# Attention with a gated MLP on one core: two more key blocks on VectorE, and another written-out order

## The chip, the core and the metric

The kernel runs on one core of a Trainium2 chip. Four compute engines work in parallel, each through its own in-order queue of instructions: TensorE (PE) multiplies matrices, ScalarE (ACT) computes exponentials, VectorE (DVE) and GpSimd (POOL) do elementwise work; SyncE (SP) issues transfers. The metric is the device time of one execution in microseconds. The time before is 680.48 us, the median of three runs (678.22 to 682.14).

## The reference

The input is x, 2048 rows of 512 values in bf16. After a layer norm, two branches are computed and added to x:

```python
xn = layernorm(x)
# A: attention, 32 heads of 16
q, k, v = heads(xn @ wqkv)
p = softmax(q @ k.T / 4)          # 2048 x 2048 for each head
A = (p @ v) @ wo
# B: gated MLP, 1792 wide
gate, up = xn @ W_gate, xn @ W_up
B = (gate * (gate > 0) * up) @ W_down
out = x + A + B
```

The attention has 32 x 2048 x 2048 exponentials, 134 million. They are the bulk of the elementwise work.

## The kernel before

**Tiles.** Queries are taken in 4 chunks of 512 (c4), heads in 4 groups of 8 (gg), and each group in two sets of 4 heads (ee). That gives 32 blocks. For each block the keys run in 16 key blocks of 128 (kt), so there are 512 key blocks in all, and each holds 4 heads x 128 keys x 512 queries of scores.

**TensorE in halves.** Nearly all matmuls are 64 rows by 32 columns of the array. A "half operation" is four such matmuls side by side on one half of the rows (lines 260 to 266); two half operations, one on each half, can run at once. Ahead of it stand its four weight loads. While the program is emitted (lines 404 to 411), the weights that each half holds are tracked: where the next half operation on the same half has the same weights (`wkey`), its loads are left out. The scores of one key block on one half share their weights (keys), and so do the products with V of the same key block on one half.

**Two ways to compute an exponential.** A key block on ACT takes 4 score half operations, into two pairs of PSUM banks that are reserved for this, two ACT instructions on 128 x 1024 values (line 1420, one "unit" each, `ring<-ps`), and two half operations on V. A key block on DVE (`quad`, line 1367 on) takes 4 score half operations into the four shared PSUM banks, four DVE instructions that add a bias and round to int16 (line 1375, `qd<-ps`), which makes the raw bit pattern of a bf16 number close to the exponential, and two more patterns of the same size, shifted by a constant, whose sum with the first comes nearer to the exponential. Each shift is one DVE instruction on 128 x 2048 values (line 1394) or two pieces on GpSimd (line 1390). All three patterns are multiplied with V, so there are six half operations on V. Raw tiles have 4 buffers, patterns 5. Scores of a key block on DVE are asked for up to 10 units ahead.

The table `QUAD_AT` has a row for each of the 32 blocks and a character for each of its 16 key blocks: a dot means ACT, a digit DVE. The digit says which shifts go to GpSimd: 0 neither, 1 the first, 2 the second, 3 both. There are 159 digits, so 353 key blocks are on ACT: 706 units. The first two blocks are done by halves: key blocks 0 to 7 of each, then 8 to 15 of each.

**Everything else** stands in the background: projections for Q, K and V, the MLP (`glu`, its products evicted at lines 1059 and 1063), and the output rows (`out_rows`). Its PSUM banks are the four shared ones. After each block its sums are copied (line 1253), inverted, and multiplied in on GpSimd (lines 1282 and 1287).

**The order.** Nothing is scheduled at run time. `PLAN` is a compressed list with one entry for each operation in the order in which all engines' queues are filled, and the buffer that each takes. `PLAN_OPS` is its length, 8302. `Graph.run` (line 339) replays it. A wait is put in wherever an operation needs one of another engine, and each engine's queue is in order: behind an instruction that waits, the rest of that queue waits too.

Of the kernel before, what the change touches and what calls it, by code (L numbers as in the profile page):

```python
# [16 lines left out]
S = 2048  # L17
D = 512
H = 32
DH = 16  # L20
F = 1792
# [3 lines left out]
NB = 4  # L25
NGG = 4
VW = 18
VN = 17
# [41 lines left out]
    ".0....3.....2...",  # L70
    ".3...3...2...3..",
# [15 lines left out]
    "3.2.3..3..2..3..",  # L87
# [32 lines left out]
NHS = 20  # L120


PLAN_OPS = 8302
PLAN = (
    "c-mcC2|!F;8@}(kGt)Fpi&QGv_dSuNLPGXPSraW}7fEHwPJ}Fd5`~n|A|X-8k}b-<@0GG;-;$Yo|8vg0cgp{vnmcECm*;)n=bY(dn1BD{$v<BDiF}b>kv|Pz;vX9_FNGh(3B2$g`71o;|5=b{s-HD@h5s?H#BHkQ"
    "OH=53;%?Qu>I@LRG<d}`4T|X;PJG0HWQS-mr!$=w=YnLYZcUyCX(wq9U^rm}(6xpCIELo{|DoeJG6d*;934V_=ER-oL{9eu-jtZela25{o)?3`>4K`WLo}8{{|1E2!n-qcJD#jZCz1yowHr8TM_w|Pz9a+bmOOCM"
    "hWHsLx=UVBk3>Itx+KpD+Y*m}r+(qE(HF!DAcpYNEi#(UqF!+%jvOP!NX&;A5*kYV-@>NUO<sJH;b<K3roam?$euzRr5N*!?x_%S;KYCn`Jsl9VDn<e=`)TlPUlKF=4h}$T!H!lf|;C<Bq7Ok4dS5|1WUzbsE>jX"
    "!XOeb2@!$^)Bz0=tQ1F(eMJkzh?1}L4Z$~tcq+avB3aD7XuA|D3F90iMutwrfT7RCN)<NNGGgSA7KwPLai$Z+y~qr$7*Ga8_l3|QI#gU=OfnuTI`~gQbmb-$U(KT9#6rWE77ZlmCMIzbWI(J_4u_itMVvukN47yi"
    "Qs@uWb%-doiFabgwLF8!7%j;I2O#<^*iV)t?*EmOy`^9XB!L7wc>E6j!_(p;Ka$`G!IKz8M44c;7Id6}?Z%ta$7D5%WFdTXDH>$0SSut~!p=0_40$4^jf6;-907O&P<bIvya+n{PlK@M0x(4EFf`?KJD%DuvH{rz"
    "n<^xm(=A4$i?^hX;D5wzPK=tsDx#IVt_R>?&{fEHvIp4-KV=XH61iw8m(cmVNP_~vNYMYt$eUV$+=KvYbsQpA6U~PRB914~$HV9o9<M_q#fu(_-1$dAfP<YOE@%;n7k(4xk(Lf8)HOAqM`8d;HiYa776@xmx2PrL"  # L130
    "J4aKA<4iXc!A)lgcoo+bs88Tc3_OBB0hvNX@fR(529<hZPKkx$It06wN*WKbNC=!+Y!Y6Hghw1nCXva%<%mW{h=O1$b&Yt&i<#yncxjP{UYbO$Fo!3sz)?EJjsq?@p^C9p40(x24bti)6-#&H88Ll$9+JvNs0x9L"
# [1345 lines left out]
```

## Time and profile before

| what | value |
|---|---|
| runs, median (lowest to highest) | 680.48 us (678.22 to 682.14) |
| profiled execution | 675.45 us |
| its span in the trace | 673.5 us |
| busy: PE, ACT, DVE, POOL | 666.5, 656.0, 616.3, 512.5 us |
| weight loads (PEld) | 381.7 us, 21226 instructions |
| matmuls | 22358 |
| granted TensorE clock | 1.0 |

The profiled execution was 5 us quicker than the median run. In the profile's lines a group is named by line, engine and operation, what it writes and reads, its shape and count; behind the bar stand its busy time in us and the mean of one in ns, and after the second bar the idle time of the engine just before it with what ended it. The mean of one counts from start to end; instructions of an engine overlap at their ends, so busy time divided by count is the step from one to the next. In the windows there is, for each engine, busy time and in brackets the number of instructions.

### The profile page before, as it was taken

What the parts mean: (1) busy time and instruction counts of PE and PEld (TensorE: products, weight loads), DVE (VectorE), ACT (ScalarE), POOL (GpSimd) and SP (SyncE); (2) the same over time, 40 slices, a digit from 0 to 9 for tenths busy, and PEclk for the clock granted to TensorE, in tenths of its full rate; (3) what the DMA queues carried; (4) which work ended last, traced back from release to release, by engine and by line L of the source; (5) the groups of instructions that cost most, each with busy time, mean ns of one, the idle gap of its engine ahead of it and who ended that gap; (6) DMA issues with size and microseconds to landing.
All of it is one profiled execution on the core that took longest, in us unless ns stands there. A gap on an engine that the chain in (4) does not pass through costs nothing.

```text
span 673.5 us, 46743 instructions
## 1 busy us (share of the span) xinstructions
PE 666.5 (99%) x22358; PEld 381.7 (57%) x21226; DVE 616.3 (92%) x1042; ACT 656.0 (97%) x718; POOL 512.5 (76%) x519
## 2 busy tenths in 40 slices
PE   8999999999999999999999999999999999999998
PEld 4545655555565556555556655565565565565554
DVE  8958889999999999989999989998999899999894
ACT  6999999999999999999999999999999999999995
POOL 3322676787788788897788877898988888898883
PEclk9999999999999999999999999999999999999999
DMA  7330121112321111112110102111121212111111
GB/s 219 52 76 24 53 64 36 42 47 79 82 80 49 52 39 37 53 51 72 47 47 23 47 5 73 25 52 52 46 58 43 55 30 55 43 32 50 46 50 49
DMA packets 57806, 35.96 MB, mean 53 GB/s; under 512 B 21196, under 2 KB 53644, under 8 KB 57612
## 3 DMA queue, kind: packets, MB, share of 16 engines
q1 hardware_dynamic: 57324, 32.72, 18.0%
q8 instruction: 170, 2.79, 1.6%
q10 hardware_dynamic: 288, 0.26, 0.1%
q14 instruction: 24, 0.20, 0.1%
HBM read 26.35 MB, written 2.35 MB: 43 GB/s over the span
## 4 chain that ended last, share of the span: by engine, by line
PE 94%; DVE 4%; DMA 1%; POOL 0%; issue 0%; ACT 0%; SPq 0%
PE ps L264 94%; DVE stats L760 1%; DVE xn_sb L773 1%; DMA xnT<-xn_sb 1%; DMA x_sb<-in_A_x_dram 0%; DVE v_aug L911 0%; DVE qT L987 0%; DVE qd L1375 0%; DVE xnT L814 0%; DVE kT L904 0%; DVE mv L761 0%; POOL rstd L755 0%; ACT xn_sb L1219 0%; DVE kT L1001 0%; SPq L689 0%
## 5 line engine op out<-in xcount | busy, mean ns | idle before, releaser
L1420 ACT ACTIVATE ring<-ps 128x1024 bf16<-128x1024 f32 x706 | 649.7, 1129 | 2.9 <-PE ps L264 2.5
L1390 POOL TENSOR_TENSOR qd<-qd,ints 128x512 int32<-128x512 int32 x458 | 462.5, 1041 | 124.9 <-DVE qd L1394 59.3
L264 PE MATMUL ps<-qT,kT 64*32 64x512 bf16 x8192 | 458.7, 374 | 0.2
L1375 DVE TENSOR_SCALAR qd<-ps 128x512 int16<-128x512 f32 x636 | 412.0, 685 | 33.5 <-PE ps L264 29.3
L264 PE MATMUL ps<-qd,v_aug 64*32 64x512 bf16 x3816 | 302.0, 375 | 0.0
L264 PE MATMUL ps<-ring,v_aug 64*32 64x512 bf16 x2824 | 242.3, 375 | 1.4 <-DVE kT L904 1.4
L1355 PEld LDWEIGHTS <-kT 64*32 64x32 bf16 x7944 | 163.8, 92 | 105.1 <-issue 14.9
L1327 PEld LDWEIGHTS <-v_aug 64*32 64x32 bf16 x5756 | 138.5, 91 | 73.4 <-issue 11.4
L264 PE MATMUL ps<-xnT,wgs 64*32 64x512 bf16 x1792 | 140.5, 374 | 0.0
L264 PE MATMUL ps<-xnT,wus 64*32 64x512 bf16 x1792 | 137.2, 374 | 0.0
L1394 DVE TENSOR_SCALAR qd<-qd 128x2048 int16<-128x2048 int16 x89 | 63.2, 715 | 0.5 <-PE ps L264 0.2
L844 PEld LDWEIGHTS <-wgs 64*32 64x32 bf16 x1792 | 43.0, 91 | 23.7 <-issue 3.5
L844 PEld LDWEIGHTS <-wus 64*32 64x32 bf16 x1792 | 43.1, 91 | 23.3 <-issue 2.1
L264 PE MATMUL ps<-Wd,hT 64*32 64x512 bf16 x608 | 54.5, 375 | 0.0
L844 PEld LDWEIGHTS <-hT 64*32 64x32 bf16 x1440 | 34.7, 92 | 19.8 <-issue 1.4
L264 PE MATMUL ps<-Wo_p,x_sb 64*32 64x512 bf16 x480 | 42.8, 375 | 0.0
L264 PE MATMUL ps<-Wv,hT 64*32 64x512 bf16 x448 | 40.9, 375 | 0.0
L1059 DVE COPY up_sb<-ps 128x512 f32<-128x512 f32 x56 | 38.3, 683 | 1.4 <-PE ps L264 0.7
L264 PE MATMUL ps<-xnT,Wq 64*32 64x512 bf16 x480 | 36.6, 375 | 0.2
L264 PE MATMUL ps<-Wv,xnT 64*32 64x512 bf16 x576 | 36.3, 374 | 0.1
L264 PE MATMUL ps<-Wk,hT 64*32 64x512 bf16 x384 | 35.5, 375 | 0.0
L264 PE MATMUL ps<-xnT,Wk 64*32 64x512 bf16 x480 | 34.0, 374 | 0.4 <-DMA xnT<-xn_sb 0.2
(73 smaller groups left out, 308.3 us busy)
## 6 DMA issues: line engine op xcount, KB each, us to landing
rb<-rec_scr SPq DMA_DIRECT2D x124, 64.0 KB, 2.2
wus<-in_B_W_up_dram SPq DMA_DIRECT2D x38, 128.0 KB, 2.8
wgs<-in_B_W_gate_dram SPq DMA_DIRECT2D x38, 128.0 KB, 2.9
xr_sb<-in_A_x_dram SPq DMA_DIRECT2D x16, 128.0 KB, 2.6
qT<-qf SPq DMA_DIRECT2D x120, 16.0 KB, 1.9
out_dram<-xn_sb SPq DMA_DIRECT2D x14, 128.0 KB, 2.3
x_sb<-in_A_x_dram SPq DMA_DIRECT2D x8, 128.0 KB, 2.9
x_sb<-oT SPq DMA_DIRECT2D x60, 16.0 KB, 2.0
```

Source lines behind the costliest of these rows:

```text
L264: return e.add_instruction(mybir.InstMatmult(name=e.bass.get_next_instruction_name(), engine=mybir.EngineType.PE, ins=[e.lower_ap(x), e.lo ...
L760: G.op("DVE", 580, lambda e, m=m: e.bn_stats(stats[:, m, :], xs(m)), reads=[t_xm[m]], writes=[t_st], prio=pr, order=last_xn if m == 4 else ())
L773: G.op("DVE", 320, lambda e, m=m, t=t_n: e.tensor_scalar(xn_sb[:, t.slot, :], xs(m), mv[:, m, 0:1], rstd[:, m:m + 1], op0=ALU.subtract, op ...
L844: e.ldweights(w()[rows, 32 * j:32 * j + 32], tile_position=(rows.start, 32 * j))
L1059: G.op("DVE", 603, lambda e: e.tensor_copy(up_sb[:, tup.slot, :], bank_of(tu)), reads=[tu], writes=[tup], prio=-590)
L1327: e.ldweights(vs(j), tile_position=(64 * half, 32 * j))
L1355: e.ldweights(ks(m), tile_position=(64 * half, 32 * m))
L1375: G.op("DVE", 601, lambda e, j=j, tx=tx: e.tensor_scalar(qd[:, tq.slot, 512 * j:512 * j + 512], ps[:, BANK[tx.slot], :], IBIAS[3], 0.0, op ...
L1390: G.op("POOL", POOL_NS / POOL_PIECES + 60, lambda e, x=x, n=n, c=slice(i * m, i * m + m): e.tensor_tensor(x().bitcast(I32)[:, c], raw().bi ...
L1394: G.op("DVE", 600, lambda e, n=n, x=x: e.tensor_scalar(x(), raw(), float(SHIFTS[n + 1]), None, op0=ALU.add), reads=[ti, tq], writes=[t], p ...
L1420: exp_ops[u] = G.op("ACT", 904, lambda e, tr=tr, k0=k0: e.activation(ring[:, tr.slot, :, :], ps[:, 4 * k0:4 * k0 + 2, :], ACTF.Exp, scale= ...
```

## The change

Two key blocks move from ACT to DVE (161 digits instead of 159, 351 key blocks on ACT, 702 units): key block 9 of block 1 and key block 7 of block 2. In block 18, key block 0 goes to ACT and key block 15 goes to DVE in its place, with one of its shifts on DVE where both were on GpSimd. The order in `PLAN` is another one throughout, with half operations of the same weights side by side more often: 1650 weight loads fewer are issued. Nothing else differs.

```diff
 QUAD_AT = (
     "................",
-    ".0....3.....2...",
-    ".3...3...2...3..",
+    ".0....3..2..2...",
+    ".3...3.2.2...3..",
     "2...3..3..0..3..",
...
     "2...3..3..0..3..",
-    "3.2.3..3..2..3..",
+    "..2.3..3..2..3.2",
     "2...2..3..0..3..",
...
-PLAN_OPS = 8302
+PLAN_OPS = 8319
 PLAN = (
...
```

More of the change, by code (lines that the diff above doesn't have):

```diff
@@ new lines @@
+    "c-m!K2S82l`#;ZnPPf}_ku+4cFIgFp8A(<p(jucMlD@K|j4xlw$S7G+D#}VInThNfg?#OujO<al_niOxzUQ2K^ZU1)&Uwc(KF{ZQp7(@d{`?Tgw;*4UAM$VHv++}W*_e4MUPu!J@frCNZwr4cC@{Kvjh^9e=9#pO"
+    "ZoWK)K9hDMAH1|LF!B}xSwvtOJ=fll#!9OQ+9mN1K_|igY$h<gG>XSxAjq51(c}xXIxzwdbc8@g;%WFdG8XWsv<kT=2=qQR7>J7jPq*L^nNF|7T|fhL44zJI3HTNgBwZOvA@UOm(j@62Sw$3*h)izqqLl<97NfnU"
+    "tJ6EO8a&;O3QL6pt<ON~AUsA8l^~k{S%@Lm^jqM?&4KPs1fmPl*+gy78cOFELB^6Gn^KS`>a5I5-;#L+x(oHUAnC$TF&IWeE~(L}n8eIlZ1Lhx(I|9=AkeW?D{)J*D-n?VrePRKO>rJiEs39K=x84PKWgZLl9B=v"
@@ new lines @@
+    "_hRT>QD@1Z8Y;3JJ46+p0!G}1ItD}|NGK9b!i(sko)b03Gt{gICh8~I4m^dBEI4(Tel>LvFIktkTgDC|vS>i7kcOI+ZZE=uNKQdbp-GjZKoEuDDKJ5U#3@KrlR^TCD5W@|Na4j8lJF_T6_rPjBUkj309u5LI24U0"
+    "&=}Lmp@PU3)Y=RZRiy}^>uV6b7N|tL0NT*kkg>8GMOPF3MVJ$}X+(L5T^L@9YwA=gEl5jJ?Zl@VVgVW2R10hj2{Ir)kTk?2#egBk6HQKk;@ugf0WGy^M9UFTM0I!yOwpQxXb@uI8V(7%fT27=Y(h04a|KB*1{e+K"
+    "sEur(!8=N{CTO%VDWj5()&OQ9@c{`2VryPTq-0=<Q?f7iKQBkHC>|o<q~<|*C{-PpDt(bGY6&E<A>jf!4n?UM(W`=n3QBh*R%NKMHAvzIvbGpkcn5kZ?k5w!XiIuqltd6&kE}*5CXy6ZMRFerL145)=&E!L4Rt=X"
@@ new lines @@
+    "n}k1XYzh;)rKG&P9i!cfF851G89@+r#iKRU`gkG(lx&bL#c6P8YGgQ&u`;5tDaaxex(xY7(sNz}HugldQbI$OzBb=!NOGav#8U&*7FRM6zD+?*9tp&2yh!21#nkB{SVdTgL?j_V40sSE_mI_z^dj_l5-U;+X^<G8"
+    "L|joB7E2{6PR9OHl50XUB(%h}#f*d`3Z?uaCu@zEK&fL8Pvs=?^TeQ{%91z51!!c5K_sRqX_!cVI35`!azB!`C49zc6_tw(jhMh?d`Lp6SwTub;s6@_f)*Xrz%)0KF>0X2ia>)^12Q|1tqGYk+LXb7nv?Si2!9kV"
+    "QltuU0+Dl{n4al<yq1VVDjAlQC4@`)lEPk$Il2=STdEqw3@g<%BFR%r@v;>Jt%Ou~neHeuDduI|syQ)gkX#*V8D1uKZ6zh830V_u6(IakJ4#xJ55%fR${0wORip|*hBmdo6a_$vEU^v}A%)}=fV34NS(BI3pPZ;g"
@@ new lines @@
+    "x+km3$&H~~NI9JcnbL&X1*TjJ$ZCtUEr<rkqp4x!GPHJyENI;-Q@c#uf?VcFGeFMt+LBZPsRRNVxr~%`CASa?5c46AWV@220Rk^mDg!i&@^bYiR(DcC!fW9n5YneI$oOQmaV8hlf=*aTj#`2WwLC4zMaCcXE$HgP"
+    "TD5@a0=dl9tuM<WbC)2dCK|=Owh-1<u+qw)p&3Og9lse<I*_tHwF6;1(O1;*JkrL!6wxw(c_cZ9*NXntxR!&oqT*S<Ik7yX7#6)H@+Z{{;duh1>pG~VWw6Nm$??HUSP;aD4&;_aswQQ!VHho9<wij)8pYH?D<rW_"
+    "BCN>Bl@owiNl27S%_Q+3uT6zw5)_ai<p9bENM~5F2;j9frXW{<bT3)}A)U5jvLZDx66ADA30q1E{8tmH!V#knNsbb2D8oUE5}IIti}{^aZxW};D5ai6YFR-+td=Bh6bTb2eW_|B{zBRki4pUNh5;SbP@<8lL)u#~"
@@ new lines @@
+    "Vj%wJNR=V?L|V|)B18#K64>N2PA>n61vMfXkXX}V+u%isvv{%51Ce&5SeNKoW?;E$q!tk&A~h9^+&kCmeu&B-*3V*(Ct6ZkM35O$%)XLVj99^m*wQkZ)cjHB@>&T+QsL!JNNkm~fh0Dd+P0dP1O_qQBm>FqnjkGK"
+    "r*F}X3|*WTLrd)4<W^tH$f7t>e=C*OQgI_642VF`-qA>HsAMZC3`Hf#_8L}O?2C4gcwgI1%j}N{K$<2yhS<CIISH?=$+a8m+$5eb2x9m3(G&^Va+*d1qNTeS<CL$Yy=e<Z&l2Ql!<7>!Rr|DIqD6~D7=lKJ3^_(c"
+    "Xi8RPpjshux0pQCpgq%(K%-0ef-V;@x{^RLopjAh4|u6bmC_RfteO{e<&U<Xl6zx8N5r&LrB7sz7x5%8AI!w)q75KMtrSM2b^)=CAnAv8?$X%=Pcyzq0NQR^cQ_%s6}0H6T}g<QFeBqz;&#b-w6)Y$1oH8LmbtX2"
@@ new lines @@
+    "Q*sT!Xc=9QPCaTL!_~^BLalQYX$v0dR+ba2cv7H4npEt`uBQATww|=-BPxpBzqXPRv<<a*Qbi*Tq*Nf6G1`8L5u0jWEHb1R0I_Wrv~9E8v1-q9wC-kT2A26)jdYcRAeJ<>C|^F;(;d`7E#%2Hn6^6>YT2CE6(@Wx"
+    "@9?^Fzgo#&d&~lIHig=ix=43OE(65?mup^Hf@mc2;VGkwXIV(QtjJ`v<fR7$QtyZZgC*^b)bEL&r}Z9>q*@S3<f=Q*k_s%bTceGqM#?FI3~NNoc2P}w`lu^TMWuhJMBU$7NF_h}XW6PNxc{d`k&!0UI;xdUQ*>vj"
+    "y7NHYQ7+BYQjtr91-@3tDrim5Gum!KTL4QZA-D%Yz-x1}sJ^7Gm<UA#5+DkkTF#a_8A%mGnpu$`c}DDb7^!`x&nYA&nirix`Io0Hy>t?x0Ua6AN{B(?DFF|EG&cgT;drUv)*hQ6B7s1OiXKJKQa}&`LOLYiC6=bW"
@@ new lines @@
+    "4brl=RQB`o=^{-Rv~xjHCY2Ar#70LRCmn|h^065sm;N&K$thZwz-7csZGt>p;%8Y^UhMGHthTCPbS=GHxXR$cHWVu=?NKs0mqgmi4hg#G(l(;nj^PhT$-IUHoOI>GK3#g}C1c7*)S|c=B%dw9Z^Veq4st^+%ETaD"
+    "6D~KPf7Iqu11X|TJbx9%7Ar=XbU=ILC!RV0Bh=;^=@gRo^tDPCTBXZ{g^vB1+VKTiv3SV}Jo872snwbb+Qt+9w<)dNuQ57Sma72ybY1QkCGOYOh|<|TFC}Hk@q+eDUyuq!=`0-Na)^i8g&&0g67y{B_f0z4cwN`2"
+    ">roh})qZQ!!k?!K+BXjW({2j7HxBZdvY>5K<eKM?bqF!a4%Bjy?yQ5Um97Or_#@rFYM?t8;X(I?ftLb9#wW1~FTIlz$ql53+CY<%xgZu&@(DM6A%be*QpzBr))H~cOay<tjggZ&BlDf0Jr$Gd27wpXV8p}B+ApaX"
@@ new lines @@
+    "-MhS6uX`BX>o?J<jG*lhbT9IRTCf&sl|0&4Tz|aLgIWolul=4y7adYM*S)gTzI)_l`wEgd<x>PkJ|3@qPR>gw;*zms<)o@#B5BFkbPcUKB=*HpQ9`U(YU|DqNgW_HG>rIyO73uZsRI`^l_4s7OD#2e@Ml>g=$igN"
+    "xJo`Y(4C_(wN7$s6;iTQ<X4SyveOQb&ZxDO@gGzuJB`=9aizC^bG2U;)FKxtF0==F+Lw@0fyT%+6!X6wfqVol_ZGDe9BcL3wK@={)(M=vrojB~dt+XQ!diD3zP6UNjLHbLDiVqHbYPZphj_LsmqhT#yD#~$n!ep*"
+    "YNs=%Rztw($V+>?$o%=DTL4{y$@~#Ug4R>oV=Ns5YSn{3^wwrT>8-M$BU1UrATO&_``x@aT>Gk5E3TNkYJJJ?rkL8!V(P)4A1@T3`27P|Kmuw5EYGt1l@1(dP|flNHPGoAr_Z*6o6xZY^vQ4wPNT2EUy8d;xrYes"
@@ L229 @@
+    "qY|SL&!A-#)`57IET+%UvW?6#)gzWyQ1$>??vV5*6)P+yLFygC9wr=31PrY$h{;HuhKndd5F8<X>Ia;Cz!<NuhaIgTo3Nl{34`DurEVa(9Ak;4#R8dOOv@n!OZ;raQY*8jv}gj#8-&&<N=b=ImM{ccVs}$)8Y5~V"
+    "hSQ^K5WX~^<p9<Q?C>BHnshNw5GtYNE3IOQrA!D%(b^LuP(_q5AZY@Tk^+Omh!nAu;3)GbNF0&-Dk>7LZHQ56Q9?!-lE_DlxfLzP2o9;tN?ZfbD5TCKg%(zdTo9z-=eWvIC@dNfBT{mvV;Sl@3M-Zo*@k8X01*j5"
+    "Qm=y6wHzfX2E>8|vHu6m;-IP")
 class Pool:
```

177 lines of the change are left out of this document (75 added, 102 removed).

## The prediction

> **What bounds the kernel now.** First the page: the totals and the costliest groups.
>
> ```profile
> span 673.5 us, 46743 instructions
> PE 666.5 (99%) x22358; PEld 381.7 (57%) x21226; DVE 616.3 (92%) x1042; ACT 656.0 (97%) x718; POOL 512.5 (76%) x519
> L1420 ACT ACTIVATE ring<-ps 128x1024 bf16<-128x1024 f32 x706 | 649.7, 1129 | 2.9 <-PE ps L264 2.5
> L1390 POOL TENSOR_TENSOR qd<-qd,ints 128x512 int32<-128x512 int32 x458 | 462.5, 1041 | 124.9 <-DVE qd L1394 59.3
> L264 PE MATMUL ps<-qT,kT 64*32 64x512 bf16 x8192 | 458.7, 374 | 0.2
> L1375 DVE TENSOR_SCALAR qd<-ps 128x512 int16<-128x512 f32 x636 | 412.0, 685 | 33.5 <-PE ps L264 29.3
> L264 PE MATMUL ps<-qd,v_aug 64*32 64x512 bf16 x3816 | 302.0, 375 | 0.0
> L264 PE MATMUL ps<-ring,v_aug 64*32 64x512 bf16 x2824 | 242.3, 375 | 1.4 <-DVE kT L904 1.4
> L1355 PEld LDWEIGHTS <-kT 64*32 64x32 bf16 x7944 | 163.8, 92 | 105.1 <-issue 14.9
> L1327 PEld LDWEIGHTS <-v_aug 64*32 64x32 bf16 x5756 | 138.5, 91 | 73.4 <-issue 11.4
> L1394 DVE TENSOR_SCALAR qd<-qd 128x2048 int16<-128x2048 int16 x89 | 63.2, 715 | 0.5 <-PE ps L264 0.2
> ```
>
> PE's 99% cannot be taken at its word, because ends of matmuls are modelled. ACT's 97% can: 706 exponentials fill 649.7 us, 0.920 us each, and ACT stands idle ahead of them for 2.9 us in the whole run. (The mean of 1129 ns overlaps with the next one; the step is what counts.) So I read ACT's timeline next, at both ends and in a quiet place.
>
> ```profile
> 11.65 13.25 ACT L1420 ACTIVATE ring<-ps 128x1024 bf16<-128x1024 f32 x14
> ...
> 299.27 4.70 ACT L1420 ACTIVATE ring<-ps 128x1024 bf16<-128x1024 f32 x5
> 299.27 5.61 ACT L1420 ACTIVATE ring<-ps 128x1024 bf16<-128x1024 f32 x6
> ...
> 649.43 14.91 ACT L1420 ACTIVATE ring<-ps 128x1024 bf16<-128x1024 f32 x16
> ```
>
> The exponentials run from 11.65 to 649.43 + 14.91 = 664.34, that is 652.7 us. Undisturbed, one more costs 5.61 - 4.70 = 0.91 us, so 706 of them need 642.5 us. What PE's lateness adds is 652.7 - 642.5 = 10.2 us in all. The rest of the span, 11.65 us ahead and 9.2 us behind, is start and tail. **ACT is the bound; PE takes the second place.** How near PE is, the timeline of its two row halves and the windows tell.
>
> ```profile
> 301.60 0.38 PE L264 MATMUL ps<-ring,v_aug 64*32 64x512 bf16 x4
> 301.61 0.38 PE L264 MATMUL ps<-qT,kT 64*32 64x512 bf16 x4
> 301.81 0.38 PE L264 MATMUL ps<-ring,v_aug 64*32 64x512 bf16 x4
> 301.82 0.38 PE L264 MATMUL ps<-xnT,wus 64*32 64x512 bf16 x4
> 302.03 0.38 PE L264 MATMUL ps<-ring,v_aug 64*32 64x512 bf16 x4
> 302.04 0.38 PE L264 MATMUL ps<-xnT,wus 64*32 64x512 bf16 x4
> ...
> 301.81 0.10 PEld L1327 LDWEIGHTS <-v_aug 64*32 64x32 bf16 x4
> 301.83 0.10 PEld L844 LDWEIGHTS <-wus 64*32 64x32 bf16 x4
> 302.03 0.10 PEld L1327 LDWEIGHTS <-v_aug 64*32 64x32 bf16 x4
> ```
>
> ```profile
> 25.00:50.00 25.00, 23.09 (x772) 12.23 (x752) 18.31 (x31) 23.61 (x26) 6.57 (x8) 1.00 0.32 66
> 50.00:75.00 25.00, 24.95 (x844) 13.93 (x816) 20.68 (x33) 25.00 (x28) 9.82 (x10) 1.00 0.13 37
> 175.00:200.00 25.00, 25.00 (x860) 14.80 (x800) 24.62 (x42) 24.98 (x28) 21.97 (x23) 1.00 0.27 74
> 225.00:250.00 25.00, 25.00 (x900) 14.34 (x804) 22.86 (x39) 24.91 (x28) 19.51 (x21) 1.00 0.13 36
> 375.00:400.00 25.00, 25.00 (x860) 14.52 (x796) 23.65 (x39) 23.75 (x26) 18.57 (x19) 1.00 0.09 22
> sum 675.00, PE 666.47 PEld 381.65 DVE 616.26 ACT 656.03 POOL 512.52; mean PE 24.68 PEld 14.14 DVE 22.82 ACT 24.30 POOL 18.98
> ```
>
> (Columns: PE, its weight loads, DVE, ACT, POOL, each with its instructions; then clock, DMA share, GB/s.) A half operation is four matmuls. Two stand side by side, one on each row half, and each half starts a new one every 0.215 us: eight matmuls in 0.215 us, 930 in 25 us. The windows have 844 to 900: PE at 91 to 97% of what it can do, at a full clock. The loads (0.10 us for four) lie under the 0.215 us of the other matmuls.
>
> **The change part by part.** The digits of the table of blocks give the counts. Block 1 gains a key block of kind 2 and so does block 2; block 18 loses one of kind 3 at its first place and gains one of kind 2 at its last. Check: a block of kind 2 issues 17 operations (4 scores, 4 evictions, 1 shift on DVE, 2 on POOL, 6 half operations on V), kind 3 issues 18, and a block on ACT 8. Two times 17 - 8, and 17 - 18 once, is +17: the plan's 8302 to 8319. None of these issues a DMA, so SP's queue has the same work.
>
> ACT: 4 exponentials fewer, 4 x 0.920 = -3.7 us (-3.6 at 0.91). This is on the path.
>
> DVE: 8 evictions at 412.0/636 = 0.648, +5.2 us; shifts 89 to 92 at 63.2/89 = 0.710, +2.1. Together 616.3 to 623.6, which in a span 4 us shorter is 93%. Where it falls: with 1.84 us for an ACT key block, key 9 of block 1 lies near 54 us and key 7 of block 2 near 74 us, their evictions up to ten exponentials (9 us) sooner. The windows from 25 and from 50 leave DVE 6.7 and 4.3 us, and one block takes 4 x 0.648 + 0.71 = 3.3. Free room covers it; without it, as in the window from 175 (24.62 of 25), 3.3 us of DVE would push evictions back and with them PE.
>
> POOL: 458 to 460 pieces at 462.5/458 = 1.01, +2.0 us where POOL is busy 10 of 25 us. Nothing. The three added shifts on DVE, however, keep POOL waiting, as 59.3 us of its idle time behind L1394 show: at 59.3/89 = 0.67 us each, 2.0 us, hidden in the same way.
>
> PE: a block on DVE has 4 scores and 6 half operations on V, one on ACT 4 and 2; two blocks more are +8 half operations, +4 on each row half, 4 x 0.215 = +0.9 us, spread thinly and in windows with 772 and 844 of 930. Block 18 begins after 288 of 512 key blocks, at 11.65 + 652.7 x 288/512 = 379 us. There ACT is busy only 23.75 of 25 us: its scores come late. Moving that block from first place to last takes four half operations (0.43 us over two halves) out of the start of this stretch and puts them behind it. I count -0.4.
>
> The order with 1650 loads fewer (21226 to 19576). The lower bound of its worth is nothing: the spacing is 0.215 us with a load for every half operation, as shown. The upper bound is all the lateness, 10.2 us. Something lies between, because loads do harm where one half has several operations in a row:
>
> ```profile
> 511.70 0.38 PE L264 MATMUL ps<-ring,v_aug 64*32 64x512 bf16 x4
> 511.91 0.38 PE L264 MATMUL ps<-qd,v_aug 64*32 64x512 bf16 x4
> 512.13 0.38 PE L264 MATMUL ps<-ring,v_aug 64*32 64x512 bf16 x4
> 512.23 0.71 PE L264 MATMUL ps<-qT,kT 64*32 64x512 bf16 x12
> ...
> 511.70 0.31 PEld L1327 LDWEIGHTS <-v_aug 64*32 64x32 bf16 x8
> ```
>
> Three times one four starts alone, 0.21 us apart, and the other half starts nothing until 512.23: each load needs its half's previous matmuls to have started, and the queue behind it waits, an exponential's scores too. Without a load a successor would not block. The Trainium skill says in "TensorE: Matmul & The Clock Gate" (Part 3, the mechanism) that a load overlaps matmuls in flight only where the row group differs; these rows agree, since the loads of that one half came one by one. Its section on the back-to-back issue gap has the spacing set by load and matmul together; at 301.60 to 302.04 the trace disagrees, 0.215 us with loads. But 1650/4 = 413 half operations without a load, of 5560, meet the lateness only in part, so 413/5277 of 10.2 us would be 0.8; as blocking runs are where the lateness is, and side-by-side order makes some runs longer, I take -0.6, near the lower bound.
>
> The order can also cost: bounded above by what the same rows let DVE wait, see the third rival. In the likeliest case I put it at nothing, with the four shared banks as cover.
>
> Sum: -3.7 - 0.4 - 0.6 = -4.7 us. The profiled execution took 675.45 us (span 673.5 and 1.95 around it), so 670.8. The median of the runs shown is 680.48, 5.0 above it; the difference carried over, 675.8 us. The likeliest case's own range is 673 to 678.
>
> **The rivals.** First, larger relief: loads and queue blocking are the main part of ACT's 10.2 us. If two thirds go, 6.8, plus 3.7: -10.5, 670 us. For it: the rows at 511.70. Against it: ACT's longest visible gap is at 375 to 400, where PE does 860 of 930 whether loads are there or not.
>
> Second, no net gain: ACT's floor sinks by 3.7 but PE, at 93%, and DVE, at 93%, come late by as much, since each exponential waits for two half operations in an in-order queue. Lateness rises from 10.2 to about 13; time 679 to 681. This includes the case in which the loads go and nothing hangs on them.
>
> Third, on the other side: putting two scores of the same keys side by side means two of the four shared banks must be free together, while DVE frees one each 0.648 us. PE's queue stands behind the second score, and the exponential's scores stand behind that.
>
> ```profile
> DVE qd L1375 <- PE ps L264: 29.3, 72, 1.0
> POOL qd L1390 <- DVE qd L1375: 37.1, 14, 18.0
> ```
>
> DVE now waits for PE 72 times, so work does not pile up in front of it; but 322 such pairs (two in each of 161 blocks) need only lose 22 ns of ACT's time each, 322 x 0.022 = 7.1 us, to eat the 3.7 and make it 0.5% slower. At 35 ns, one wait of a full eviction in every nineteen pairs, it is +11.3 - 3.7 = +7.6: 688 us. That the three streams on V start together, only when the last pattern from POOL is there, acts alike, but has 4 raw and 5 pattern buffers as cover.
>
> **How the numbers follow.** Half a per cent (3.4 us) is about what a measurement of this kernel can tell from no change. Likeliest case 0.40, larger relief 0.14, no net gain 0.20, slower 0.26. The likeliest at -4.7 stays beyond -3.4 for nearly all its range; I leave 0.02 of it to no change: faster 0.52, same 0.22, slower 0.26. The range from 668 to 688 leaves out the top of the first rival (0.05) and the dearer half of the third (0.13).
>
> **What would show it.** Counts: 702 exponentials, 644 evictions, 92 shifts on DVE, 460 pieces on POOL, about 19576 loads. Right: the exponentials' run from first start to last end falls from 652.7 to about 648, and ACT fills 24.2 or more of the window round 379. Wrong: that run is 650 or more with ACT's wait for PE above 2.9 us, or DVE's 33.5 us of idle time grows together with it (third rival), or the windows from 25 to 75 lose what DVE had free. A first exponential later than 11.65 or a tail longer than 9.2 us would be a cause outside all of this.

## The result, and the profile after

The kernel after takes 674.92 us (median of six runs, 673.84 to 676.23), the kernel before 680.33 us beside it (six runs, 678.22 to 682.14). The ratio is 0.9926, with an interval of 0.9902 to 0.9951: faster by 5.4 us, where 4.7 were forecast. In a later session the same two kernels gave 673.52 and 676.85 us, a ratio of 0.9957 (0.9942 to 0.9973), so 2.9 us by the ratio. Which chip the first measurement ran on is not on record. Neither interval reaches 1, so the gain is clear of noise in both, and the forecast lies between them.

The page of the kernel after, its totals and groups:

```profile
span 674.0 us, 45117 instructions
PE 664.3 (99%) x22387; PEld 371.8 (55%) x19578; DVE 620.8 (92%) x1053; ACT 653.9 (97%) x714; POOL 514.2 (76%) x521
L1420 ACT ACTIVATE ring<-ps 128x1024 bf16<-128x1024 f32 x702 | 647.6, 1088 | 6.9 <-PE ps L264 5.9
L1390 POOL TENSOR_TENSOR qd<-qd,ints 128x512 int32<-128x512 int32 x460 | 464.1, 1039 | 120.7 <-DVE qd L1394 80.1
L1375 DVE TENSOR_SCALAR qd<-ps 128x512 int16<-128x512 f32 x644 | 416.1, 684 | 29.6 <-PE ps L264 26.2
L1394 DVE TENSOR_SCALAR qd<-qd 128x2048 int16<-128x2048 int16 x92 | 65.6, 718 | 0.3
```

The counts are those of the forecast (two loads more, 19578). The rest of these lines is harder to read than it looks. The profiled execution of after took 675.82 us; that of before took 675.45 us, less than any of its six timed runs. So the first pair of traces shows none of the gain: exponentials busy 2.1 us less (647.6 against 649.7), but waiting 4.0 us more (6.9 against 2.9). To compare traces I therefore took a second one of each kernel in the later session (below). Its spans are 675.3 for before and 673.5 for after.

Two windows of after that answer to those shown of before, one of early work and one of the stretch round block 18 (columns as before: PE, weight loads, DVE, ACT, POOL):

```profile
50.00:75.00 25.00, 25.00 (x853) 14.07 (x776) 23.17 (x39) 23.40 (x26) 12.81 (x13) 1.00 0.11 28
375.00:400.00 25.00, 25.00 (x872) 14.36 (x744) 22.56 (x37) 25.00 (x29) 20.57 (x21) 1.00 0.18 51
```

ACT is busy 1.6 us less in the early window (25.00 to 23.40) and 1.25 us more in the late one (23.75 to 25.00). What fills the late one is seen in ACT's timeline. First before, then after; each row is an unbroken run of exponentials, with its start, its length, their number and the gap ahead of it:

```profile
373.41 3.90 ACT L1420 ACTIVATE ring<-ps 128x1024 bf16<-128x1024 f32 x4
377.58 5.61 ACT L1420 ACTIVATE ring<-ps 128x1024 bf16<-128x1024 f32 x6 [0.28 <-PE ps L264]
383.53 3.77 ACT L1420 ACTIVATE ring<-ps 128x1024 bf16<-128x1024 f32 x4 [0.34 <-PE ps L264]
387.81 4.69 ACT L1420 ACTIVATE ring<-ps 128x1024 bf16<-128x1024 f32 x5 [0.51 <-PE ps L264]
```

```profile
372.97 19.45 ACT L1420 ACTIVATE ring<-ps 128x1024 bf16<-128x1024 f32 x21
...
654.67 11.11 ACT L1420 ACTIVATE ring<-ps 128x1024 bf16<-128x1024 f32 x12
```

Block 18's first exponential starts at about 389 us in both kernels. The three gaps ahead of it, where before, up to 10 units early, asks for the scores of that block's first key block on DVE, are gone in after. The last row gives the end of the exponentials, 654.67 + 11.11 = 665.78, and with it a tail of 674.0 - 665.78 = 8.2 us, 0.9 less than before's 9.2.

One more part of the page counts, and the prediction never used it: the summary of the chain of waits, the shares of the span by engine. Before, then after:

```profile
PE 94%; DVE 4%; DMA 1%; POOL 0%; issue 0%; ACT 0%; SPq 0%
```

```profile
PE 82%; ACT 12%; DVE 4%; DMA 1%; POOL 0%; SPq 0%; issue 0%; ACTq 0%
```

ACT, which the prediction called the bound, is on 0% of the chain before. Its 12% after is not a lasting trait of that kernel, as the second trace of after shows:

```profile
PE 90%; DVE 5%; DMA 2%; ACT 1%; SPq 1%; issue 0%; POOL 0%; ACTq 0%
```

The experiments are about what sets the pace.

### The profile page after: what moved, and what is told of

Its sections match the earlier page's. It is cut to its first block, busy times and chain, and to the rows that moved or that the text cites. A ratio compares the mean times of both kernels' runs of the same rounds, so it can differ in the third digit from the quotient of the medians.

```text
span 674.0 us, 45117 instructions
## 1 busy us (share of the span) xinstructions
PE 664.3 (99%) x22387; PEld 371.8 (55%) x19578; DVE 620.8 (92%) x1053; ACT 653.9 (97%) x714; POOL 514.2 (76%) x521
## 4 chain that ended last, share of the span: by engine, by line
PE 82%; ACT 12%; DVE 4%; DMA 1%; POOL 0%; SPq 0%; issue 0%; ACTq 0%
PE ps L264 82%; ACT ring L1420 12%; DVE stats L760 1%; DVE qd L1375 1%; DMA rsum<-o_sb 1%; DVE v_aug L911 1%; DVE xn_sb L773 0%; DMA x_sb<-in_A_x_dram 0%; DVE qT L987 0%; DVE mv L761 0%; DVE xnT L814 0%; ACT xn_sb L1219 0%; DVE kT L904 0%; POOL rstd L755 0%; DVE rrec L1270 0%
## 5 line engine op out<-in xcount | busy, mean ns | idle before, releaser
L1420 ACT ACTIVATE ring<-ps 128x1024 bf16<-128x1024 f32 x702 | 647.6, 1088 | 6.9 <-PE ps L264 5.9
L1390 POOL TENSOR_TENSOR qd<-qd,ints 128x512 int32<-128x512 int32 x460 | 464.1, 1039 | 120.7 <-DVE qd L1394 80.1
L1375 DVE TENSOR_SCALAR qd<-ps 128x512 int16<-128x512 f32 x644 | 416.1, 684 | 29.6 <-PE ps L264 26.2
L264 PE MATMUL ps<-qd,v_aug 64*32 64x512 bf16 x3864 | 276.1, 375 | 0.0
L264 PE MATMUL ps<-ring,v_aug 64*32 64x512 bf16 x2808 | 230.3, 375 | 0.0
L1355 PEld LDWEIGHTS <-kT 64*32 64x32 bf16 x7544 | 158.7, 92 | 118.2 <-issue 30.3
L1327 PEld LDWEIGHTS <-v_aug 64*32 64x32 bf16 x4508 | 108.9, 92 | 55.7 <-issue 7.9
L264 PE MATMUL ps<-xnT,wgs 64*32 64x512 bf16 x1792 | 137.2, 374 | 0.0
L264 PE MATMUL ps<-xnT,wus 64*32 64x512 bf16 x1792 | 135.5, 375 | 0.0
L1394 DVE TENSOR_SCALAR qd<-qd 128x2048 int16<-128x2048 int16 x92 | 65.6, 718 | 0.3
L844 PEld LDWEIGHTS <-hT 64*32 64x32 bf16 x1440 | 35.2, 92 | 20.8 <-issue 2.7
```

Source lines behind the costliest of these rows:

```text
L264: return e.add_instruction(mybir.InstMatmult(name=e.bass.get_next_instruction_name(), engine=mybir.EngineType.PE, ins=[e.lower_ap(x), e.lo ...
L844: e.ldweights(w()[rows, 32 * j:32 * j + 32], tile_position=(rows.start, 32 * j))
L1327: e.ldweights(vs(j), tile_position=(64 * half, 32 * j))
L1355: e.ldweights(ks(m), tile_position=(64 * half, 32 * m))
L1375: G.op("DVE", 601, lambda e, j=j, tx=tx: e.tensor_scalar(qd[:, tq.slot, 512 * j:512 * j + 512], ps[:, BANK[tx.slot], :], IBIAS[3], 0.0, op ...
L1390: G.op("POOL", POOL_NS / POOL_PIECES + 60, lambda e, x=x, n=n, c=slice(i * m, i * m + m): e.tensor_tensor(x().bitcast(I32)[:, c], raw().bi ...
```

## The experiments

Two theories to begin with. The prediction's: ACT paces the run, each exponential taken away is worth 0.92 us, and the loads next to nothing. The rival: PE's queue with its waits paces the run, time taken from ACT alone comes back as waiting, and the gain is the order's, by its fewer loads or otherwise. All ratios are to the kernel before in the same session. It took 676.85 us beside the first eight kernels, on one chip, and 676.70 us beside the last four (thin exponentials, the two halves of the order, the moved transfer), on another chip.

**Each kernel once more.** The kernel before and the kernel after, unchanged.

> The kernel before once more, for a second trace of it. The first profiled execution took 675.45 us, its six other runs 678.22 to 682.14. If that trace was a lucky one, this one's span is 677 to 680 us and the exponentials' run, first start to last end, is 656 to 659 us instead of 652.7; the lateness of PE (that run less 706 x 0.91 us) is then some 14 to 16 us, and the order has more to win than the prediction gave it. If the profile itself makes the difference, the span is 673 to 675 us again.

> The kernel after once more, beside the other runs of this study: the half-width and reload runs are to be read against it. If the loads are worth nothing, its ratio to the kernel before lies at 0.996 to 0.998, as that of the run with 412 loads put back (0.9968). If they carry the gain, it lies at 0.991 to 0.994.

Before gave 677.0 us, ratio 0.9997 (0.9981 to 1.0012), with a span of 675.3 us and an exponentials' run of 655.0 us in its trace, between its two cases. After gave 673.52, ratio 0.9957 (0.9942 to 0.9973), nearer to the case in which the loads are worth nothing. These two traces are the base of what follows.

**ACT alone, at the place of the change.** Eight exponentials of the kernel before, at or beside the two key blocks that the change moves, are halved: the other half of their columns is left out.

```diff
-e.activation(ring[:, tr.slot, :, :], ps[:, 4*k0:4*k0 + 2, :], ACTF.Exp, scale=EXP_SCALE)
+n = 1 if key in ((0,0,1,8), (0,0,1,9), (0,1,0,7), (0,1,0,8)) else 2
+e.activation(ring[:, tr.slot, 0:n, :], ps[:, 4*k0:4*k0 + n, :], ACTF.Exp, scale=EXP_SCALE)
```

> The kernel before, its order untouched, with 8 exponentials of half the width (512 of 1024 columns; the other half of what they should compute is left out) where the change takes its blocks from ACT: about 8 x 0.43 = 3.4 us of ACT work less, with 0.43 us estimated from the 0.920 us of a whole one and 0.59 us of an ACT instruction on 512 columns. Theory (ACT is the bound): 3 to 4 us faster, ratio 0.994 to 0.996. Rival (the gain comes from the order, PE is late anyway): under 1 us, ratio 0.9985 to 1.001.

676.61 us, ratio 0.9997 (0.9983 to 1.0011): nothing, where 3 to 4 us were at stake. Where they went stands in ACT's timeline at one of these places, and in ACT's row of the waits (us in total, times, longest), first of this kernel, then of the kernel before again:

```profile
49.56 5.82 ACT L1420 ACTIVATE ring<-ps 128x1024 bf16<-128x1024 f32 x7
55.65 0.60 ACT L1420 ACTIVATE ring<-ps 128x512 bf16<-128x512 f32 x1 [0.27 <-PE ps L264]
56.65 0.60 ACT L1420 ACTIVATE ring<-ps 128x512 bf16<-128x512 f32 x1 [0.40 <-PE ps L264]
57.49 19.08 ACT L1420 ACTIVATE ring<-ps 128x1024 bf16<-128x1024 f32 x21 [0.24 <-PE ps L264]
```

```profile
ACT ring L1420 <- PE ps L264: 6.7, 19, 1.2
```

```profile
ACT ring L1420 <- PE ps L264: 3.3, 8, 1.2
```

The seven of the first row include two short ones, at 54.09 and 54.79 us, so four are short here. The two shown alone are over in 0.60 us, and then ACT waits for the next scores. From the first of the four to the next full one at 57.49 it takes 3.40 us, 0.85 each, where four full ones take 3.7. ACT's wait for PE grew by 3.4 us, about all that was cut. The scores were not there earlier, but for some 0.3 us here, and so ACT's 0.91 us step was nearly the step of PE's scores as well.

**ACT alone, spread, in the kernel after.** Sixteen exponentials, one in 44, are halved (`n = 1 if u % 44 == 20 else 2` in the same place).

> The kernel after with 16 exponentials of half the width (the other half is left out), one in 44 units: 16 x 0.43 = 6.9 us of ACT work less, spread over the run. If ACT is the bound all along: 6 to 7 us faster than the kernel after, ratio to the kernel before 0.982 to 0.984. If PE or DVE binds elsewhere: 1 to 4 us, ratio 0.987 to 0.991.

673.27 us, ratio 0.9945 (0.9925 to 0.9966), against 0.9957 for after itself in the next session on the same chip. The difference of 0.8 us is inside both intervals.

**ACT alone, everywhere.** In the kernel before, every exponential from the 65th on has 1000 columns instead of 1024; the other 24 are left out.

```diff
-e.activation(ring[:, tr.slot, :, :], ps[:, 4*k0:4*k0 + 2, :], ...)
+n = 500 if u >= 64 else 512
+e.activation(ring[:, tr.slot, :, 0:n], ps[:, 4*k0:4*k0 + 2, 0:n], ...)
```

> The kernel before with every exponential from the 65th on over 1000 instead of 1024 columns (the other 24 are left out): 642 x 24 x 0.8 ns = 12 us of ACT work less, evenly, with 0.8 ns a column from the 1063 and 654 ns that 1024 and 512 columns take in the run with half-width ones. If ACT paces the run: 9 to 12 us faster, ratio 0.982 to 0.987. If PE's frozen order with its own waits needs as long as ACT: under 4 us, 0.994 to 1.0.

675.34 us, ratio 0.9982 (0.9971 to 0.9992): about 1.2 us. Taking 24 of 1024 columns off 642 exponentials would be worth some twelve if ACT set the pace. The row of the thin ones, then that of the kernel before again (a trace from the other chip):

```profile
L1420 ACT ACTIVATE ring<-ps 128x1000 bf16<-128x1000 f32 x642 | 587.0, 1014 | 5.2 <-PE ps L264 3.8
```

```profile
L1420 ACT ACTIVATE ring<-ps 128x1024 bf16<-128x1024 f32 x706 | 651.0, 1102 | 4.0 <-PE ps L264 3.3
```

The mean of one falls by 88 ns, from 1102 to 1014, though only 2.3% of its columns are gone (the kernel before alone has 1129 in its first trace and 1102 in its second), and the step only from 651.0/706 = 0.922 to 587.0/642 = 0.914 us. A duration here thus holds time in which the instruction overlaps its predecessor or waits, and a row without idle time is no proof that its engine is the bound. The Trainium skill, "Perfetto Trace Analysis" (Identifying the Most-Contended Engine), takes the share of busy time of Vector, Scalar and GpSimd for a fair measure of how close one is to the roofline. It has the engine with the highest share optimized first. ACT, at 97%, has the highest of these three, and these runs disagree: 2.3% less of its work gave 0.18% of the time.

**PE alone, DVE alone, all three.** In the kernel before, about 125 half operations on V at half width (`n = 256`, every 13th but a stream's first and last), then 26 of 636 evictions at half width (`nd1 % 24 == 12`), then both together with sixteen halved exponentials, one in 44. What the other half would have computed is left out.

```diff
+pv:        n = 256 if npv % 13 == 0 and 0 < st[0] < st[1] - 1 else 512
+eviction:  n = 256 if nd1 % 24 == 12 and nd1 > 24 else 512
```

> The kernel before with about 125 half operations on V at half width (256 of 512 queries of their product are left out), spread over the run: 125 / 2 x 0.107 = 6.7 us less on each row half. If PE alone binds: 5 to 7 us faster, ratio 0.990 to 0.993. If PE only follows ACT or DVE: under 1.5 us, 0.998 to 1.0. If the three pace each other in a fixed order, as the half-width exponentials without effect suggest: some of it, 1 to 3 us.

> The kernel before with 26 evictions at half width (the other half of their block's rounding is left out), spread over the run: 26 x 0.27 = 6.9 us of DVE work less, 0.27 us estimated as two fifths of the 0.65 us of a whole one. If DVE alone binds: 5 to 7 us faster, ratio 0.990 to 0.993. If it does not: under 1 us. If the three pace each other: 1 to 3 us.

> The kernel before with all three cuts at once, 16 exponentials, 26 evictions and about 125 half operations on V at half width: 6.7 to 6.9 us less on each of ACT, DVE and PE. If the three pace each other: 4 to 7 us faster, ratio 0.990 to 0.994, clearly more than any cut alone. If one engine alone binds, no more than that engine's own cut. If waits for transfers and latencies of the order bind, under 2 us.

676.76 us, ratio 1.0002 (0.9991 to 1.0012) for PE; 676.12 us, 0.9994 (0.9984 to 1.0004) for DVE; 675.03 us, 0.998 (0.9969 to 0.9992) for all three. So PE's own work does not set the step either: some 6.7 us less of it on each row half gave nothing, though PE has 94% of the chain before. No engine alone is worth anything clear of noise here at this size. A cut on all three gives 1.4 us by its ratio, where 4 to 7 were expected if the three paced each other. It cannot be told from the sum of the cuts made alone: 0.4 us for DVE, 0.8 for the sixteen exponentials in the kernel after, none for PE. Under 2 us is the case in which waits for transfers and the latencies of the order bind. Which of them do is not shown. That PE waits for scores' banks and patterns that the others hold, in a queue whose order is fixed, is a reading that no run here singles out.

**The loads.** In the kernel after, 412 of the half operations that reuse weights load them again, which makes as many loads as before; the order stays.

```diff
 elif held[o.half] == o.wkey:
-    o.load, o.wsrc = False, ()
+    same += 1
+    if same * 412 // 703 == (same - 1) * 412 // 703:
+        o.load, o.wsrc = False, ()
```

> The kernel after, its order untouched, with 412 of the 703 half operations that reuse weights loading them again, spread evenly: as many loads as before (21226), 1648 more than after. Theory of the prediction (loads lie under matmuls, only runs on one half suffer): 0 to 1 us slower than after, ratio to the kernel before 0.9925 to 0.994. Rival (loads bind PE): 4 x 0.024 = 0.10 us for each of 206 on a half, up to 20 us, ratio 1.00 and above; a third of this would be 0.999.

674.47 us, ratio 0.9968 (0.9954 to 0.9982), against 0.9957 (0.9942 to 0.9973) without. The totals of this kernel, then of after again:

```profile
PE 663.9 (99%) x22387; PEld 392.5 (58%) x21226; DVE 620.1 (92%) x1053; ACT 654.1 (97%) x714; POOL 515.1 (77%) x521
```

```profile
PE 664.2 (99%) x22390; PEld 370.7 (55%) x19578; DVE 620.2 (92%) x1053; ACT 653.9 (97%) x714; POOL 515.2 (76%) x521
```

21.8 us more of loads leave PE, DVE, ACT and POOL where they were. The 1648 loads are worth 0.7 us by the ratios, with zero well inside. This trace happens to be 0.9 us shorter than that of after again.

**The order cut in two.** One kernel takes after's order, with its two added key blocks on DVE, to the last exponential of block 7 (about 187 us) and before's from there; the other takes before's first and after's from there, with block 18's change.

```diff
 QUAD_AT:  first: rows 1 and 2 of after, row 18 of before; second: the other way round
-PLAN = (...)      # one order
+PLAN = (...)      # one order up to exponential (0, 3, 1, 15), the other's remaining entries behind it
```

> A splice: the order of the kernel after up to the last exponential of block 7 (near 187 us), with its two added blocks on VectorE, and from there on the order of the kernel before, block 18 as before. 161 blocks on VectorE, 304 loads fewer. Theory (the two blocks are the gain, as the traces read key by key say, less what the late transfers of sums cost near 140 us): 1 to 3 us faster than before, ratio 0.9955 to 0.9985. Rival (the loads, or the rest of the order, are the gain): 0.999 to 1.001.

> The other splice: the order of the kernel before up to the last exponential of block 7, and from there on the order of the kernel after, block 18 as after. 159 blocks on VectorE, 1340 loads fewer. Theory (block 18's moved block gives about 2 us near 380 us and the tail up to 1 us, of which late transfers near 185 us and PE's stops at 417 us take back 1 to 2; the loads give nothing): 0 to 2 us faster, ratio 0.997 to 1.0. Rival (the loads carry the gain, four fifths of them are here): 0.9965 or below, and the pace between key blocks 320 and 510 quicker than before.

682.23 us, ratio 1.0077 (1.0056 to 1.0098), and 677.41 us, 1.0012 (1.0003 to 1.0021), both slower than before. Neither half gives the gain, and the two don't add up to it (+0.77% and +0.12%, against -0.43% on the other chip). Both lose their time behind the seam (the table below, key blocks 129 to 273). For the first half the chain of waits shows it:

```profile
192.77 0.46 SPq L1274
...
194.20 3.07 DMA rb<-rec_scr
...
197.34 1.28 POOL x_sb L1282
...
199.57 4.48 POOL qd L1390 x4
...
204.10 6.97 PE ps L264 x198
```

The broadcast of the inverted sums (`rb`, line 1274) stands behind a row of SP's issues that both orders brought to this place. POOL takes it before its next pattern pieces, PE waits for these, and the exponentials for PE. So these two say little of the change, and where the second half loses its time I did not find.

**The wait that the new order made.** A wait appears in the traces of after that before does not have: DVE's reciprocal of the sums for their transfer. DVE's row of the waits from 120 to 190 us in after (us in total, times, longest), then the chain of after:

```profile
DVE rrec L1270 <- DMA rsum<-o_sb: 3.6, 2, 3.0
```

```profile
139.44 0.43 SPq L1046
139.88 0.04 issue
139.92 2.09 DMA rsum<-o_sb
142.01 0.02 issue
142.03 0.26 DVE rrec L1270
142.29 0.54 DVE qd L1375
142.83 0.60 DVE kT L904
...
143.48 16.58 PE ps L264 x514
```

SP issues the transfer of the sums at 139.92, when DVE is nearly at the reciprocal; DVE stands still for 3.0 us, the keys' copy and then PE behind it. In the repair, the order lets the transfer into SP's queue right behind the copy of the sums, and ten reciprocals come at least five DVE instructions later.

```diff
 copy of the sums to o_sb (line 1253)
+transfer rsum <- o_sb (line 1269)
 ... other transfers of SP
-transfer rsum <- o_sb (line 1269)
```

> The kernel after with one thing moved: each block's transfer of its sums is queued right behind the copy that makes them, ahead of the weight transfers, and ten reciprocals that stood less than five VectorE instructions behind that transfer stand five behind it. Theory (VectorE's wait for this transfer, 2.0 to 3.0 us near 140 us and 0.8 to 1.2 near 185 us, stops PE and ACT in the kernel after): that wait is gone and the kernel is 1 to 3 us faster than after, ratio to the kernel before 0.9915 to 0.9945 where after has 0.9957. Rival (the wait only takes the place of others): 0.995 to 0.997.

679.13 us, ratio 1.0034 (1.002 to 1.0048): slower than after and than before. The wait is gone; the reciprocal near 141 us follows DVE's previous instruction without a gap:

```profile
140.68 0.68 DVE L1394 TENSOR_SCALAR qd<-qd 128x2048 int16<-128x2048 int16 x1
141.28 0.24 DVE L1270 RECIPROCAL rrec<-rsum 128x16 f32<-128x16 f32 x1
```

But each transfer that is moved up is moved past others. SP's timeline of the repaired kernel near 420 us, then its chain of waits there, then SP of after again:

```profile
417.48 0.60 SPq L1269 DMA_DIRECT2D rsum<-o_sb  x1
418.12 2.95 SPq L894 DMA_DIRECT2D qT<-qf  x3
421.12 2.17 SPq L1274 DMA_DIRECT2D rb<-rec_scr  x4
```

```profile
422.99 2.64 DMA rb<-rec_scr
...
425.76 0.04 POOL oT L1287
...
426.99 1.05 POOL qd L1390
...
428.08 21.95 PE ps L264 x735
```

```profile
417.15 3.21 SPq L1274 DMA_DIRECT2D rb<-rec_scr  x4
420.73 1.25 SPq L894 DMA_DIRECT2D qT<-qf  x2
422.04 0.59 SPq L1269 DMA_DIRECT2D rsum<-o_sb  x1
```

The sums' transfer now waits at the head of SP's queue for its copy, and the previous block's broadcast, which went out at 417.15, goes out at 421.12. POOL's multiplication waits for that broadcast, its pattern pieces behind it are late, and PE waits for them. By the table below this kernel loses 3.1 us between key block 321 and the end. Its traced execution, 676.46 us, was the second fastest of its twelve, 2.7 us below their median, so these rows show one place of the loss and not all of it.

**Where the time lies.** To see the places, I took from each trace the start of the first exponential of a key block on ACT, the key blocks numbered 0 to 511 in the order of work, and subtracted that of the kernel before again. Negative is ahead, in us; the last column is the difference of the spans.

| trace | key block 42 (80 us) | 97 (150) | 129 (188) | 273 (368) | 321 (429) | 511 (664) | span |
|---|---|---|---|---|---|---|---|
| after, first trace | -2.7 | +0.3 | +0.9 | +1.1 | 0.0 | -0.4 | -1.3 |
| after again | -1.8 | +0.1 | +0.9 | +0.3 | -0.4 | -0.8 | -1.8 |
| after, loads as before | -2.6 | -2.4 | -1.2 | -1.5 | -2.3 | -2.3 | -2.7 |
| after, sums' transfer moved | -2.7 | -2.4 | -2.4 | -1.9 | -2.8 | +0.3 | -0.7 |
| after's start, before's rest | -3.5 | -2.5 | -1.8 | +2.6 | +2.6 | +2.5 | +2.5 |
| before's start, after's rest | 0.0 | 0.0 | 0.0 | +2.2 | +1.4 | +1.3 | +0.8 |
| before, thin exponentials | -0.8 | -1.0 | -1.0 | -1.8 | -2.0 | -2.1 | -2.1 |
| before, 8 halved | -0.4 | -0.5 | +0.1 | -0.2 | -0.1 | 0.0 | 0.0 |

One execution differs from the next by 1 to 2 us (the first trace of before would end at -1.8), so only steps that all rows of a kind share can be used. These are: 1.8 to 3.5 us ahead by key block 42 in every trace with after's start; 2 to 3 us lost between 42 and 97, and 0.6 to 0.8 more by 129, in both traces of after, where the transfer of the sums is late. The two kernels that had no wait for it near 140 us (loads as before, transfer moved) keep their lead to 97, and the one with the transfer moved keeps it to 129; but one trace with before's order, eight halved, loses 0.6 us from 97 to 129 too. Then 0.7 to 1.1 us are won between 273 and 321 in the five traces with block 18's change, and from 321 to the end there is no difference of pace between the orders that is larger than that between two traces of before, whatever loads they have, but for the repair's losses. The tail then gives 0.9 to 1.0 us in both traces of after and in the repair, and 0.4 to 0.5 in the other two kernels that end with after's order.

The start has two steps to itself. ACT's timeline of after again, then of before again:

```profile
49.86 13.95 ACT L1420 ACTIVATE ring<-ps 128x1024 bf16<-128x1024 f32 x15 [0.27 <-PE ps L264]
64.16 1.94 ACT L1420 ACTIVATE ring<-ps 128x1024 bf16<-128x1024 f32 x2 [0.35 <-PE ps L264]
66.54 1.02 ACT L1420 ACTIVATE ring<-ps 128x1024 bf16<-128x1024 f32 x1 [0.44 <-PE ps L264]
68.13 32.30 ACT L1420 ACTIVATE ring<-ps 128x1024 bf16<-128x1024 f32 x35 [0.57 <-PE ps L264]
```

```profile
41.08 59.27 ACT L1420 ACTIVATE ring<-ps 128x1024 bf16<-128x1024 f32 x64 [0.21 <-PE ps L264]
```

From 29 us to the end of these rows at 100 us, after has 73 exponentials and before 75; as after needs four fewer to come as far, it is two of them ahead, which is the lead of 1.8 us. And three waits for PE stand at 64 to 68 us, in the window in which DVE went from 20.68 to 23.17 of 25 us, where before runs unbroken.

## Why the prediction was right, and where it was not

**The number and the sign: right, the number in part by luck.** 675.8 us were forecast and 674.92 measured, in the likeliest case's own range of 673 to 678. The counts came as worked out, and ACT fills the window round 379 us (25.00). But the rest of the test that the prediction itself set fails, and its sign of being wrong is met: the exponentials' run is 665.78 - 11.29 = 654.5 us in the first trace (654.0 in the second, against 655.0 for before again), not about 648, and ACT's wait for PE is 5.9 us, not under 2.9. By that test the mechanism is not as told. The number came out by terms that the prediction did not have or sized otherwise, some of which cancel.

**The second rival's mechanism is nearer to the traces.** It had PE and DVE come late by as much as ACT's floor sinks. Lateness, the exponentials' run less 0.91 us for each, was 10.2 us in the first trace of before and is 654.5 - 702 x 0.91 = 15.7 us in that of after. In the second pair it goes from 655.0 - 642.5 = 12.5 to 654.0 - 638.8 = 15.2 us, so 2.7 of the 3.6 us taken off ACT's floor came back. The rival's time, 679 to 681 us, was not met all the same.

**"ACT is the bound; PE takes the second place": wrong.** This is the step that failed. Taking time from ACT alone, 3.4 us at the place of the change or some twelve over the run, gave 0 and 1.2 us; the 3.4 us came back as waits for PE. The reading behind it was that ACT stood idle for only 2.9 us and its step was 0.91 us. Both are true and neither shows the bound, since PE's scores came at nearly that step. The chain of waits, in which ACT has 0%, would have raised the doubt; it stood on the page and was not read. It does not name the bound either: PE has 94% of it, and less work for PE alone gave 1.0002. What sets the pace stays open.

**"4 exponentials fewer, -3.7 on the path": the size was met at its place, for another reason.** Every trace with after's start is 1.8 to 3.5 us ahead by 80 us. As halved exponentials gave nothing there, it is not ACT's time that was saved. A key block moved to DVE takes two places out of the sequence in which PE feeds ACT, which a shorter exponential does not; that this is what gives the lead is argued and not shown. How much of the lead is these places and how much the new order of the start could not be told apart: the kernel meant for it was spoilt by its seam.

**"Free room covers" DVE's 7.3 us: mostly.** DVE's busy time rose by 4.5 us (616.3 to 620.8). The three gaps at 64 to 68 us, 1.4 us in all, show that not all of it was covered. In the whole run DVE's waits for PE did not grow (29.6 us of idle time ahead of the evictions, 33.5 before). POOL's idle time behind the shifts on DVE (L1394) rose by 20.8 us, from 59.3 to 80.1, where 2.0 were reckoned; its idle time ahead of these pieces as a whole fell, from 124.9 to 120.7.

**Block 18, -0.4: right in place, undersized.** Five traces give 0.7 to 1.1 us. The block's first exponential starts at 389 us and not at 379, and the crowded stretch is the one ahead of it. DVE's work in the window from 375 fell as well, from 23.65 to 22.56 us; whether that or the four half operations on PE relieved ACT was not tried.

**Loads, -0.6: not distinguishable from zero.** 0.7 us by the ratios, and no change of pace over the 235 us after key block 321, where before issues 678 loads more than after in the second pair of traces. The first rival, in which loads and blocking are the main part of ACT's lateness, finds nothing for it in these runs. The lower bound, a load lying under the other matmuls, was the better end. The rule that the prediction took from the Trainium skill's "TensorE: Matmul & The Clock Gate" (Part 3, the mechanism), that a load overlaps only matmuls of another row group, is not contradicted by this; what such loads cost hardly shows in the time.

**The order at nothing: wrong in parts that nearly cancel.** The prediction bounded it by pairs of scores held behind PSUM banks. No trace shows that; DVE's wait for PE fell, from 29.3 to 26.2 us. What the traces show lies in a queue it counted at no cost, SP's, where the late transfer of the sums took back 2 to 3 us near 140 us and perhaps some 0.6 more near 184; and at the end in a tail shorter by 0.9 us, which no term had.

**What is open.** The steps seen in the second pair of traces add up to 1.8 us, the timed runs of that session give 2.9 by the ratio and those of the first 5.4. The traced execution of after again, 675.36 us, was the slowest of its six, which is part of it. Why the gain differs between the sessions was not tried. Neither the two moved key blocks nor the new order ran alone without a seam, so how the gain divides between them is not shown. Nor is it known what made the second half of the order lose 2 us behind the seam.

## What to carry to other kernels

An engine that is 97% busy with hardly any idle time need not be the one that sets the pace, and neither need the one with 94% of the chain of waits: take a few per cent off the instructions of each before counting every instruction saved as time. Where an order is written out for all queues at once, a transfer moved earlier is moved past others in its issue queue: list what stands behind it, and who needs that, before it is moved. One execution's trace can differ from the next by more than the effect; compare steps that several traces share.

## What the runs showed of the hardware that was not expected

The mean duration of an exponential in the profile is no measure of its work: 24 columns of 1024 fewer lowered it by 88 ns, from 1102 to 1014, while the step from one to the next fell by 8 ns; and two traces of the kernel before have 1129 and 1102 ns at steps of 0.920 and 0.922 us. And 1648 weight loads more, 21.8 us of busy time, left PE's busy time at 663.9 us against 664.2.
